# Splitting gate's weight pairs while val's values are scanned, folding the second block from the first slot, and a smaller background share

## The chip, the cores and the metric

The kernel runs on one core of a Trainium2 chip. The metric is device microseconds of one execution; the kernel before has a median of 902.73 us over three runs (901.56 to 907.99).

## What is computed

Attention with a local mask in half of the heads and a strided mask in the other half gives 2304 tokens of 512 numbers. Two networks follow, one after the other:

```python
h = x @ w_in                                  # 512 -> 2048
y = (h * np.cos(h)) @ w_out                   # 2048 -> 512
g, val = y @ w_gate, y @ w_val                # 512 -> 1536, twice
out = (g / (1 + np.exp(-g)) * val) @ w_out2   # 1536 -> 512
```

The weights come as 64-bit floats. A product is made of three 16-bit matmuls, high x high, high x low and low x high, so every weight and every activation is first scaled by a power of two and split into a high and a low 16-bit half. The scale of a whole matrix must be known before its first piece can be split, so each matrix is read twice: a scan for its largest magnitude, then the split.

## The kernel before, in words

The tokens are in five blocks of 512, 512, 512, 384 and 384. The attention comes first (about 110 us). The first network then goes tile by tile, 16 tiles of 128 hidden columns in each block; I call the 80 tiles **slots** 0 to 79. In slot s TensorE (PE) runs the projection of tile s (`up1`, 12 matmuls into a PSUM bank) and one or two contractions of earlier tiles (`down1`, 12 matmuls each). The lag between them falls from 12 tiles to 2 over slots 14 to 39, and in slots 17, 19, 22, 24, 27, 29, 32, 34, 37 and 39 two contractions are run. For each tile VectorE (DVE) has two fixed operations: L577 (in the slot after the projection) and L584 (in the slot after that), which frees the bank. The banks are four. At the end of a block, DVE and ScalarE (ACT) move the four sums out of PSUM (L555 and L557).

Everything else that DVE, ACT and GpSimd (POOL) do in these slots is **background work** for the second network. It lies in one first-in first-out list (`fill`); each entry has a cost in us, and `pump` takes entries while a credit lasts that each slot refills with a share of (PE work of the slot - 1.25): `SHARE` in blocks 0 and 1, `SHARE2` after. Work on the scales and splits of the activations goes through a second list, `urgent`, one piece at each call of `pump_urgent`. The background work, in order:

- split of w_out (`direct_later`), scan of the twelve tiles of w_gate (L174), scan of the twelve of w_val (L174), each followed by `top_later`;
- `open_weights`: from the slot on in which the lag and the storage allow it, `scale_later` for both matrices, then `pair_later` for six pairs of tiles. A pair has a gate half and a val half (`pair_half`). For each half two tiles are converted (L224 on ACT, L231 and L235 on DVE), POOL forms four combinations of the two (L915), and the results are split into a high half (L245, ACT) and a low half (L248, DVE) and stored to DRAM (L863, from the SP queue). The last of seven results is shared by gate and val. The storage is eight **units**, `unit_free`, handed round in the order in which they come free;
- scan of w_out2, its scale, its split (`seven_later`).

A scale is found in `common_scale` (L136 on PE, L137 on DVE): a 128x128 matmul spreads the column maxima over the partitions into a PSUM bank of the same ring of four that `up1` uses, and DVE reduces it. The engines take their instructions in program order, so what stands behind L137 on DVE, or behind L136 on PE, waits with it.

The second network takes 30 slots of its own (`slots`, six of each block). Its operand is **folded** first: `fold_pieces` makes sums of quarters of the block (L611) and splits seven operands (L245, L248), eight pieces in the `urgent` list. For block 1 they are put there at the end of its second slot (j == 1 of block 0), and three calls of `pump_urgent` in each slot take them from slot 2 of this network on.

Of the kernel before, what the change touches and what calls it, by code (L numbers as in the profile page):

```python
# [58 lines left out]
XM = 5  # L59
HOMES, LATE, UNIT = 24, 4, 16  # L60
W7S = 3
SHARE, SHARE2, SB = 0.95, 0.85, 2


WHERE = [((q, c), (3 + q, c)) if q < 3 else ((6, 0), (6, 256))
# [14 lines left out]
def build(tc, qk_l, qk_s, v_l, v_s, w_in, w_out, w_gate, w_val, w_out2, mask_l, mask_s, eye32, eye16, out):  # L80
    nc = tc.nc
    wide = w_in.dtype != F32
    with ExitStack() as ctx:
# [65 lines left out]
        for k, a in MATS.items():  # L149
# [1 line left out]
        scale_w = {}  # L151

        order = deque([("in", j) for j in range(M1)] + [("out", j) for j in range(M1)] * 2
                      + [(mat, j) for mat in ("gate", "val") for j in range(M2)]
                      + [(mat, 2 * j + i) for j in range(NPR) for mat in ("gate", "val") for i in range(2)]
                      + [("out2", j) for j in range(M2)] * 2)

        def load_raw():
# [85 lines left out]
        def hi_part(dst, src, s):  # L244
            nc.scalar.activation(out=dst, in_=src, func=AF.Copy, scale=s)  # L245

        def lo_part(dst, src, s, hi):
            nc.vector.scalar_tensor_tensor(out=dst, in0=src, scalar=s, in1=hi, op0=ALU.mult, op1=ALU.subtract)  # L248
# [31 lines left out]
        def scan_later(mat, j, cost=0.63):  # L280
            later(cost, lambda: scan_raw(mat, j))
# [3 lines left out]
        def top_later(mat):  # L285
            begin([])
            later(0.6, lambda: tops.__setitem__(mat, spread_tops(parts_w[mat], wide)))

        def scale_later(mat, bound):
            later(0.6, lambda: scale_w.__setitem__(mat, common_scale(tops[mat], bound)))  # L290
# [571 lines left out]
        def store_home(j, q, i):  # L862
            nc.sync.dma_start(out=w7_d[j][:, q], in_=homes[i])  # L863
            unit_free.append(i)
# [3 lines left out]
        def flush_after():  # L868
            while after:
                begin(after.popleft())  # L870

        def pair_later(j):

            last = {}
            for mi, mat in enumerate(("gate", "val")):
                pair_half(j, mi, mat, last)

            def hi():
                last["h"] = unit_free.popleft()
                for mi, mat in enumerate(("gate", "val")):  # L880
                    c = slice(256 * mi, 256 * mi + 256)
                    hi_part(homes[last["h"]][:, 0, c], last["f"][:, c], scale_w[mat][0])

            def lo():
                h = homes[last["h"]]
                for mi, mat in enumerate(("gate", "val")):
                    c = slice(256 * mi, 256 * mi + 256)
                    lo_part(h[:, 1, c], last["f"][:, c], scale_w[mat][0], h[:, 0, c])
                unit_free.append(last["i"])
                store_home(j, 6, last["h"])  # L890

            after.append([(0, hi), (1.0, lo)])

        def pair_half(j, mi, mat, last):
            at, f, to = {}, {}, {}
            left, right = slice(0, 256), slice(256, 512)

            def place(q):
                at[q] = unit_free.popleft()
                f[q] = as_f32(homes[at[q]])  # L900
                return f[q]

            def combine(k):
                if k == 0:
                    place(2)
                if k == 3 and not mi:
                    last["i"] = unit_free.popleft()
                    last["f"] = as_f32(homes[last["i"]])
                op, out, a, b = (
                    lambda: (ALU.add, f[2][:, left], f[1][:, left], f[1][:, right]),  # L910
                    lambda: (ALU.subtract, f[1][:, left], f[0][:, left], f[1][:, left]),
                    lambda: (ALU.subtract, f[2][:, right], f[2][:, left], f[0][:, left]),
                    lambda: (ALU.subtract, last["f"][:, 256 * mi:256 * mi + 256], f[0][:, right], f[2][:, right]),
                )[k]()
                nc.gpsimd.tensor_tensor(out=out, in0=a, in1=b, op=op)  # L915

            def hi(q):
                to[q] = unit_free.popleft()
                hi_part(homes[to[q]][:, 0], f[q], scale_w[mat][0])

            def lo(q):
                h = homes[to[q]]
                lo_part(h[:, 1], f[q], scale_w[mat][0], h[:, 0])
                unit_free.append(at[q])
                store_home(j, 3 * mi + q, to[q])

            for q in range(2):
                steps = conv_steps(mat, 2 * j + q, lambda q=q: place(q), False)[1]
                begin(steps + [(0, lambda k=k: combine(k)) for k in range(4)] * q)
                if not q:  # L930
                    flush_after()
            parts = [[(0, lambda q=q: hi(q)), (0.7, lambda q=q: lo(q))] for q in range(3)]
            begin(parts[0])
            after.extend(parts[1:])

        def open_weights(lag):

            if lag + 4 <= UNIT:
                most[0] = UNIT
            if not opened and most[0] == UNIT and max(taken, default=0) < UNIT:  # L940
                opened.append(True)
                scale_later("gate", TW_IN)
                scale_later("val", TW_IN)
                for j in range(NPR):
                    pair_later(j)
                flush_after()
                begin([])
                later(0, lambda: None, "pairs")
                for i in range(M2):
                    scan_later("out2", i, 1.0)  # L950
                top_later("out2")
            if len(opened) == 1 and lag < LATE and max(taken, default=0) < LATE:
                opened.append(True)
                most[0] = LATE
                for i in range(3):
                    later(1.0, lambda: None)
                scale_later("out2", TW_LAST)
                seven_later()
# [2 lines left out]
        for j in range(M1):  # L961
            direct_later("out", j, wo)
        direct_end()
        for mat in ("gate", "val"):
            for j in range(M2):
                scan_later(mat, j, 1.7)
            top_later(mat)
        urgent = deque()

        def urge(pieces, key=None):  # L970
# [188 lines left out]
            return p  # L1159

        px = open_slot(0)
        for s, (blk, j) in enumerate(slots):
            n = BLOCKS[blk][1]
            h = n // 2
# [33 lines left out]
            py = halves(pacc.tile([128, 512], F32, name=f"acc{KC - 1}"), h)  # L1198
            multiply(1, w, x, py, h, True)
            join(0, 0, py, a)  # L1200
            if last:
                piece_sums(last)
                his, los = second_set(last)
                run(his)
            pz = halves(bank(), h)
            multiply(4, w, x, pz, h, True)
            b = snap(pz)
            if last:
                run(los)
            pump_urgent()  # L1210
# [26 lines left out]
            pump_urgent()  # L1237
            multiply(3, w, x, old, h, False)
            nc.scalar.activation(out=c["C"][1][:, :, 0:h], in_=old, func=AF.Copy)
            if j == 1 and blk + 1 < NBLK:  # L1240
                urge(fold_pieces(blk + 1, sy, ys, spans), ("ys", blk + 1))
            if blk == 1 and j == 2:
                urge(late_scale)
# [78 lines left out]
```

## Time and profile before

| | us |
|---|---|
| median of three runs | 902.73 |
| the profiled execution, whole | 904.13 |
| its span, first to last instruction | 902.2 |
| PE busy in the span | 862.4 |
| DVE busy | 691.8 |
| ACT busy | 521.2 |
| POOL busy | 199.3 |

The span is what the views below cut up; the 1.9 us around it are not the kernel's instructions. Busy times are sums over stretches with different limits. In a row of the timeline the first number is the start in us from the span's start, the second the duration; a bracket gives the idle time of that engine just before and what ended it.

### The profile page before, as it was taken

To read this page: it belongs to the slowest core of one execution; us is meant where nothing else is said; L and a number is where in the kernel's file an instruction comes from. 1 tells how busy PE (TensorE), PEld (TensorE's weight loads), DVE (VectorE), ACT (ScalarE), POOL (GpSimd) and SP (SyncE) were. 2 spreads that over 40 slices of the span, in tenths; PEclk is the share of its full clock that TensorE was granted. 3 is DMA by queue.
4 is the path that set the end of the run, shared out by engine and by line. 5 is a ranking of instruction groups with operands and counts; after the bars stand their busy time and mean duration, and the time that the engine had idled before them with its cause. 6 is when DMAs were issued, how large, how long until landed. Compare 5 with 4: busy or idle time off the path is not lost.

```text
span 902.2 us, 18542 instructions
## 1 busy us (share of the span) xinstructions
PE 862.4 (96%) x7228; PEld 609.8 (68%) x7228; DVE 691.8 (77%) x1337; ACT 521.2 (58%) x1046; POOL 199.3 (22%) x253
## 2 busy tenths in 40 slices
PE   7999999989999979899999998899999999999998
PEld 4776644434444434455655686788888899999998
DVE  4797989896758999869988378857886776776672
ACT  4787988763445667547887355536444444544440
POOL 3342414121234656522322200000000000000000
PEclk8897999999999989999999999999999999999999
DMA  9997751568545675651645344657677687888894
GB/s 302 352 304 219 249 187 48 163 189 272 191 144 197 214 241 178 225 204 49 215 136 198 156 151 177 247 200 265 233 255 267 216 273 284 299 290 309 317 330 148
DMA packets 53512, 200.61 MB, mean 222 GB/s; under 512 B 5456, under 2 KB 16208, under 8 KB 49584
## 3 DMA queue, kind: packets, MB, share of 16 engines
q1 hardware_dynamic: 53424, 199.42, 64.8%
q8 instruction: 57, 0.93, 0.5%
q14 instruction: 31, 0.25, 0.1%
HBM read 175.41 MB, written 23.99 MB: 221 GB/s over the span
## 4 chain that ended last, share of the span: by engine, by line
PE 66%; DVE 10%; ACT 7%; DMA 6%; issue 6%; POOL 4%; SPq 0%; POOLq 0%; ACTq 0%; DVEq 0%
PE acc L693 14%; PE bank L541 10%; PE bank L543 10%; PE bank L542 10%; PE acc L541 5%; PE acc L543 5%; PE acc L542 5%; DMA vl<-v_l 3%; PE bank L435 2%; DVE arena L248 2%; POOL arena L915 2%; POOL arena L589 2%; PE po L488 2%; ACT arena L245 2%; DMA v_pair<-v_s 1%
## 5 line engine op out<-in xcount | busy, mean ns | idle before, releaser
L541 PE MATMUL bank<-xs,wi 128*128 128x256 f16 (+3 forms) x780 | 233.8, 300 | 22.1 <-DVE tb L584 9.1
L543 PE MATMUL bank<-xs,wi 128*128 128x256 f16 (+3 forms) x780 | 234.1, 300 | 0.0
L542 PE MATMUL bank<-xs,wi 128*128 128x256 f16 (+3 forms) x780 | 233.9, 300 | 0.0
L589 POOL TENSOR_TENSOR arena<-tb,arena 128x512 f16<-128x512 f32 (+1 forms) x80 | 91.7, 1148 | 240.6 <-ACT arena L588 205.7
L542 PEld LDWEIGHTS <-wi 128*128 128x128 f16 x880 | 86.2, 98 | 62.5 <-issue 30.2
L541 PE MATMUL acc<-arena 128*128 128x512 f16 (+1 forms) x320 | 114.7, 358 | 0.0
L542 PE MATMUL acc<-arena 128*128 128x512 f16 (+1 forms) x320 | 114.5, 358 | 0.0
L543 PE MATMUL acc<-arena 128*128 128x512 f16 (+1 forms) x320 | 114.5, 358 | 0.0
L541 PEld LDWEIGHTS <-wi 128*128 128x128 f16 x880 | 86.3, 98 | 38.4 <-issue 4.1
L543 PEld LDWEIGHTS <-wi 128*128 128x128 f16 x880 | 86.3, 98 | 35.6 <-issue 1.4
L693 PEld LDWEIGHTS <-arena 128*128 128x128 f16 x1080 | 100.7, 98 | 8.2
L678 POOL TENSOR_TENSOR wi<-tb 128x256 f32<-128x256 f32 (+1 forms) x30 | 20.2, 675 | 347.5 <-DVE tb L659 347.5
L663 ACT ACTIVATE arena<-tb 128x256 f16<-128x256 f32 (+3 forms) x59 | 28.9, 489 | 115.3 <-DVE tb L659 111.6
L574 ACT ACTIVATE tb<-bank,quarter,c 128x512 int32<-128x512 f32 (+1 forms) x75 | 54.4, 725 | 49.5 <-PE bank L543 36.9
L542 PEld LDWEIGHTS <-arena 128*128 128x128 f16 x600 | 58.8, 98 | 35.0 <-issue 2.5
L693 PE MATMUL acc<-arena 128*128 128x256 f16 (+1 forms) x702 | 82.0, 265 | 0.0
L543 PEld LDWEIGHTS <-arena 128*128 128x128 f16 x600 | 58.7, 98 | 33.0 <-issue 0.2
L541 PEld LDWEIGHTS <-arena 128*128 128x128 f16 x600 | 58.8, 98 | 32.8 <-ACT arena L588 0.3
L658 DVE SCALAR_TENSOR_TENSOR tb<-tb,arena 128x512 f32<-128x512 f32 (+1 forms) x60 | 38.0, 634 | 44.9 <-ACT tb L652 44.8
L588 ACT ACTIVATE arena<-tb 128x512 f16<-128x512 f32 (+1 forms) x80 | 46.5, 581 | 35.4 <-PE acc L543 32.4
L541 PE MATMUL bank<-xs,arena 128*128 128x256 f16 (+1 forms) x240 | 62.9, 262 | 1.7 <-DVE arena L1190 1.2
L543 PE MATMUL bank<-xs,arena 128*128 128x256 f16 (+1 forms) x240 | 62.9, 262 | 0.0
(146 smaller groups left out, 1734.5 us busy)
## 6 DMA issues: line engine op xcount, KB each, us to landing
wi<-w SPq DMA_DIRECT2D x20, 1792.0 KB
arena<-w SPq DMA_DIRECT2D x60, 576.0 KB, 5.3
raw<-w_out SPq DMA_DIRECT2D x56, 512.0 KB, 4.0
arena<-w SPq DMA_DIRECT2D x10, 1792.0 KB
raw<-w_gate SPq DMA_DIRECT2D x24, 512.0 KB, 4.6
raw<-w_val SPq DMA_DIRECT2D x24, 512.0 KB, 4.4
w<-arena SPq DMA_DIRECT2D x42, 256.0 KB, 2.1
raw<-w_in SPq DMA_DIRECT2D x16, 512.0 KB
```

The costliest lines, as they stand in the source:

```text
L245: nc.scalar.activation(out=dst, in_=src, func=AF.Copy, scale=s)
L248: nc.vector.scalar_tensor_tensor(out=dst, in0=src, scalar=s, in1=hi, op0=ALU.mult, op1=ALU.subtract)
L541: nc.tensor.matmul(out=o, lhsT=w[:, 0, c], rhs=x[0], start=first, stop=False, **kw)
L542: nc.tensor.matmul(out=o, lhsT=w[:, 0, c], rhs=x[1], start=False, stop=False, **kw)
L543: nc.tensor.matmul(out=o, lhsT=w[:, 1, c], rhs=x[0], start=False, stop=last, **kw)
L574: nc.scalar.activation(out=c["w"].bitcast(I32), in_=c["ph"], func=AF.Identity, scale=turn[c["blk"]], bias=quarter)
L588: nc.scalar.activation(out=g[:, 0, 0:n], in_=w, func=AF.Copy)
L589: nc.gpsimd.tensor_tensor(out=g[:, 1, 0:n], in0=w, in1=g[:, 0, 0:n], op=ALU.subtract)
L658: nc.vector.scalar_tensor_tensor(out=t, in0=t, scalar=1.0, in1=gate, op0=ALU.add, op1=ALU.mult)
L663: nc.scalar.activation(out=to, in_=src, func=AF.Copy, scale=2.0 ** -11)
L678: nc.gpsimd.tensor_tensor(out=t_sums[:, 0, 0:h], in0=c["t"][0][:, h:2 * h], in1=c["t"][0][:, 0:h], op=ALU.subtract)
L693: nc.tensor.matmul(out=o[:, c], lhsT=w[:, 256 * i + 128 * c:256 * i + 128 * c + 128], rhs=unit(u)[:, x:x + h], start=j == c == i == 0, sto ...
```

## The change

1. `load_raw`'s order and the background list: w_val is no longer scanned ahead of the opening. When the opening comes, gate's scale is found and gate's six halves are split, with one val scan put after the first and one after the second tile of each half; then val's scale, then val's six halves.
2. `half_later` takes the place of `pair_later` and `pair_half`: the seventh result of a pair is split and stored for gate and for val apart (256 columns each; six more stores).
3. The fold of block 1 is put in `urgent` before the first slot of the second network, and that slot has three more calls of `pump_urgent`.
4. `SHARE2` goes from 0.85 to 0.75.

```diff
-SHARE, SHARE2, SB = 0.95, 0.85, 2
+SHARE, SHARE2, SB = 0.95, 0.75, 2
...
-                      + [(mat, j) for mat in ("gate", "val") for j in range(M2)]
-                      + [(mat, 2 * j + i) for j in range(NPR) for mat in ("gate", "val") for i in range(2)]
+                      + [("gate", j) for j in range(M2)]
+                      + [(mat, j) for j in range(M2) for mat in ("gate", "val")] + [("val", j) for j in range(M2)]
...
+            def last_hi():
+                last["h"] = unit_free.popleft()
+                hi_part(homes[last["h"]][:, 0, mine], last["f"][:, left], scale_w[mat][0])
+
+            def last_lo():
+                h = homes[last["h"]]
+                lo_part(h[:, 1, mine], last["f"][:, left], scale_w[mat][0], h[:, 0, mine])
+                unit_free.append(last["i"])
+                nc.sync.dma_start(out=w7_d[j][:, 6, :, mine], in_=h[:, :, mine])
+                unit_free.append(last["h"])
+
             for q in range(2):
                 steps = conv_steps(mat, 2 * j + q, lambda q=q: place(q), False)[1]
                 begin(steps + [(0, lambda k=k: combine(k)) for k in range(4)] * q)
                 if not q:
                     flush_after()
+                elif beside:
+                    scan_later(beside, 2 * j)
             parts = [[(0, lambda q=q: hi(q)), (0.7, lambda q=q: lo(q))] for q in range(3)]
             begin(parts[0])
-            after.extend(parts[1:])
+            if beside:
+                scan_later(beside, 2 * j + 1)
+            after.extend(parts[1:] + [[(0, last_hi), (0.5, last_lo)]])
...
                 scale_later("gate", TW_IN)
+                for j in range(NPR):
+                    half_later(j, 0, "gate", "val")
+                flush_after()
+                top_later("val")
                 scale_later("val", TW_IN)
                 for j in range(NPR):
-                    pair_later(j)
+                    half_later(j, 1, "val")
...
-        for mat in ("gate", "val"):
-            for j in range(M2):
-                scan_later(mat, j, 1.7)
-            top_later(mat)
+        for j in range(M2):
+            scan_later("gate", j, 1.7)
+        top_later("gate")
...
         px = open_slot(0)
+        urge(fold_pieces(1, sy, ys, spans), ("ys", 1))
...
             join(0, 0, py, a)
+            if not s:
+                pump_urgent()
+                pump_urgent()
...
             b = snap(pz)
+            if not s:
+                pump_urgent()
...
-            if j == 1 and blk + 1 < NBLK:
+            if j == 1 and 0 < blk < NBLK - 1:
```

The instructions themselves show where things go. Before, on DVE in slot 30, the scales of gate and val are found one behind the other (s_3308 is gate's, s_3317 val's; parts and xy belong to the block scales), and the first conversion of a gate tile follows:

```order
L112 RECIPROCAL s_3308<-q 128x1
L113 TENSOR_SCALAR inv_3309<-q 128x1
L114 TENSOR_SCALAR s_3308<-s_3308 128x1
L137 TENSOR_REDUCE q<-bank 128x1
L112 RECIPROCAL s_3317<-q 128x1
L113 TENSOR_SCALAR inv_3318<-q 128x1
L114 TENSOR_SCALAR s_3317<-s_3317 128x1
L231 TENSOR_SCALAR arena<-arena 128x512
L577 SCALAR_TENSOR_TENSOR tb<-bank,c_2528,tb 128x512
```

Now gate's scale stands in slot 25, and val's in slot 34, on DVE behind a scan, four low halves and L584. This is DVE's slot 34 (s_3609 is a block scale that stands in slot 34 before too, s_3057 gate's, s_3646 val's):

```order
L577 SCALAR_TENSOR_TENSOR tb<-bank,c_3439,tb 128x512
L137 TENSOR_REDUCE q<-bank 128x1
L112 RECIPROCAL s_3609<-q 128x1
...
L174 TENSOR_REDUCE pw_val<-raw 128x1
L248 SCALAR_TENSOR_TENSOR arena<-arena,s_3057 128x512 x2
L584 SCALAR_TENSOR_TENSOR tb<-tb,bank 128x512
L248 SCALAR_TENSOR_TENSOR arena<-arena,s_3057 128x512
L248 SCALAR_TENSOR_TENSOR arena<-arena,s_3057 128x256
...
L137 TENSOR_REDUCE q<-bank 128x1
L112 RECIPROCAL s_3646<-q 128x1
```

The two moved: from slot 30, where they stood together, gate's scale went five slots up and val's four slots down, with the whole of gate's split between them.

In the second network, DVE's first slot before (L1190 adds two products, L658 and L659 make the gated value, L666 a low half):

```order
L1190 TENSOR_TENSOR arena<-acc_5710,cv 128x2x256
L521 TENSOR_REDUCE parts_3_5174<-xy_69 128x1
L1190 TENSOR_TENSOR arena<-bank,cv 128x2x256
L120 TENSOR_REDUCE m<-parts_3_5174 128x1
L128 TENSOR_SCALAR p<-m 128x1
L130 TENSOR_SCALAR tops<-id_76,p 128x128
L1190 TENSOR_TENSOR arena<-bank,cv 128x2x256
L658 SCALAR_TENSOR_TENSOR tb<-tb,arena 128x512
```

and the same slot now, where the additions are L1188:

```order
L1188 TENSOR_TENSOR arena<-acc_5716,cv 128x2x256
L521 TENSOR_REDUCE parts_3_5177<-xy_69 128x1
...
L130 TENSOR_SCALAR tops<-id_76,p 128x128
L137 TENSOR_REDUCE q<-bank 128x1
...
L611 TENSOR_TENSOR wi<-xy_67 128x512
L1188 TENSOR_TENSOR arena<-bank,cv 128x2x256
L611 TENSOR_TENSOR wi<-xy_67,wi 128x512
L248 SCALAR_TENSOR_TENSOR xs<-xy_67,s_4477,xs 128x512
L1188 TENSOR_TENSOR arena<-bank,cv 128x2x256
L658 SCALAR_TENSOR_TENSOR tb<-tb,arena 128x512
```

A block scale that was spread over slots 0 and 1 is now whole in slot 0, and the first pieces of the fold stand between the additions of slot 0.

## Rows read from the trace of the kernel before

**Rows 1.** The page, part 1: busy us of each engine, share, instructions.

```profile
PE 862.4 (96%) x7228; PEld 609.8 (68%) x7228; DVE 691.8 (77%) x1337; ACT 521.2 (58%) x1046; POOL 199.3 (22%) x253
```

**Rows 2.** Windows: length, busy of PE, PEld, DVE, ACT, POOL, granted clock, DMA, GB/s.

```profile
226.98:285.15 58.17, 57.47 (x268) 26.11 (x267) 40.40 (x76) 27.80 (x46) 17.52 (x19) 1.00 0.53 183
233.03:260.44 27.41, 27.08 (x128) 12.35 (x127) 18.79 (x41) 11.07 (x19) 6.38 (x5) 1.00 0.52 192
285.15:381.17 96.02, 84.44 (x386) 38.01 (x386) 90.22 (x136) 64.44 (x108) 58.56 (x56) 0.96 0.61 206
331.00:335.00 4.00, 4.00 (x11) 1.37 (x10) 3.97 (x8) 4.00 (x8) 3.38 (x4) 0.55 0.80 265
```

**Rows 3.** Waits of PE: us in total, times, longest.

```profile
PE bank L541 <- DVE tb L584: 9.1, 6, 3.0
PE bank L541 <- DVE q L137: 6.6, 8, 3.0
```

**Rows 4.** Timeline of PE: first matmul of slots 26, 35, 41, 50 and 52.

```profile
226.98 0.38 PE L541 MATMUL bank<-xs,wi 128*128 128x512 f16 x1
...
285.15 0.38 PE L541 MATMUL bank<-xs,wi 128*128 128x512 f16 x1 [0.38 <-DVE q L137]
...
330.87 0.58 PE L541 MATMUL bank<-xs,wi 128*128 128x512 f16 x1 [3.03 <-DVE q L137]
...
381.17 0.33 PE L541 MATMUL bank<-xs,wi 128*128 128x384 f16 x1
...
390.85 0.32 PE L541 MATMUL bank<-xs,wi 128*128 128x384 f16 x1 [0.38 <-DVE q L137]
```

**Rows 5.** Timeline of DVE: around the openings of slots 26, 40 and 52.

```profile
231.06 0.75 DVE L555 TENSOR_SCALAR xy<-acc,c 128x512 f32<-128x512 f32 x1 [6.64 <-PE acc L543]
...
233.03 0.74 DVE L577 SCALAR_TENSOR_TENSOR tb<-bank,c,tb 128x512 f32<-128x512 f32 x1
...
329.87 0.74 DVE L577 SCALAR_TENSOR_TENSOR tb<-bank,c,tb 128x512 f32<-128x512 f32 x1
...
330.53 0.28 DVE L137 TENSOR_REDUCE q<-bank 128x1 f32<-128x128 f32 x1
...
396.25 0.61 DVE L577 SCALAR_TENSOR_TENSOR tb<-bank,c,tb 128x384 f32<-128x384 f32 x1
```

**Rows 6.** Groups of DVE by line and form, 260 to 375 us: count, busy, mean ns.

```profile
L248 DVE SCALAR_TENSOR_TENSOR arena<-arena,s 128x512 f16<-128x512 f32 x36 | 35.3, 993 | 6.6 <-ACT arena L245 6.3
L235 DVE SCALAR_TENSOR_TENSOR arena<-raw,arena 128x512 int32<-128x512 int32 x24 | 21.2, 882 | 0.7
L231 DVE TENSOR_SCALAR arena<-arena 128x512 int32<-128x512 int32 x24 | 14.7, 613 | 1.6 <-ACT arena L224 1.6
...
L584 DVE SCALAR_TENSOR_TENSOR tb<-tb,bank 128x512 f32<-128x512 f32 x16 | 10.8, 676 | 0.0
L248 DVE SCALAR_TENSOR_TENSOR arena<-arena,s 128x256 f16<-128x256 f32 x11 | 6.6, 637 | 0.0
```

**Rows 7.** Groups of DVE by line and form, 200 to 260 us: val's scan.

```profile
L174 DVE TENSOR_REDUCE pw_val<-raw 128x1 f32<-128x512 f32 x12 | 7.8, 675 | 0.0
```

**Rows 8.** Timeline of POOL and DVE: a low half beside POOL, one without.

```profile
322.55 3.87 POOL L915 TENSOR_TENSOR arena<-arena 128x256 f32<-128x256 f32 x4
322.57 1.26 DVE L248 SCALAR_TENSOR_TENSOR arena<-arena,s 128x512 f16<-128x512 f32 x1
...
327.49 0.74 DVE L248 SCALAR_TENSOR_TENSOR arena<-arena,s 128x512 f16<-128x512 f32 x1
```

**Rows 9.** Timeline of DVE: first addition of the second network's slots 2, 5, 6.

```profile
538.84 0.68 DVE L1190 TENSOR_TENSOR arena<-acc,cv 128x512 f32<-128x512 f32 x1
...
574.76 0.68 DVE L1190 TENSOR_TENSOR arena<-acc,cv 128x512 f32<-128x512 f32 x1
...
584.57 0.68 DVE L1190 TENSOR_TENSOR arena<-acc,cv 128x512 f32<-128x512 f32 x1
```

**Rows 10.** The page, part 6: stores of split weights, KB each, us to landing.

```profile
w<-arena SPq DMA_DIRECT2D x42, 256.0 KB, 2.1
```

More of the change, by code (lines that the diff above doesn't have):

```diff
@@ L870, in flush_after, with half_later @@
                 begin(after.popleft())
[L872 to L895, printed above, removed]
+        def half_later(j, mi, mat, beside=None):
+            at, f, to, last = {}, {}, {}, {}
             left, right = slice(0, 256), slice(256, 512)
+            mine = slice(256 * mi, 256 * mi + 256)
             def place(q):
@@ L905, in combine @@
                     place(2)
-                if k == 3 and not mi:
+                if k == 3:
                     last["i"] = unit_free.popleft()
@@ L912, in combine @@
                     lambda: (ALU.subtract, f[2][:, right], f[2][:, left], f[0][:, left]),
-                    lambda: (ALU.subtract, last["f"][:, 256 * mi:256 * mi + 256], f[0][:, right], f[2][:, right]),
+                    lambda: (ALU.subtract, last["f"][:, left], f[0][:, right], f[2][:, right]),
                 )[k]()
```

## The prediction

> **What bounds the kernel now.** I read the page's busy times first: PE is busy for 862.4 of 902.2 us [rows 1], so all that any change of order can win is some 40 us, and only where PE waits. The waits of PE come next: they name DVE, by L584 (the bank of an older tile is not free yet, 9.1 us in all) and by L137 (a scale is being found in a bank that the next projection needs, 6.6 us) [rows 3]. Third, the timeline of PE, cut at the first matmul of a slot, says where [rows 4]. Slots 26 to 34 take from 226.98 to 285.15, 58.17 us with PE busy for 57.47 [rows 2]: nine projections and thirteen contractions (four slots have two), 22 groups of 12 matmuls, so a group of 512 columns takes 57.0 / 22 = 2.59 us, after two waits for scales. Slots 35 to 49 are thirteen projections and fifteen contractions of 512 columns and two projections of 384 (slots 48 and 49 contract 512-column tiles still): 28 x 2.59 + 2 x (1.94 + 2.59) = 81.6 us. They took 96.0 [rows 2, 4]. These 14.4 us are the largest loss of the kernel. DVE is busy for 90.2 of them. In the 27 us before the first split of a gate pair, 233 to 260, it is busy for 18.8 only [rows 2]. So the idle DVE time lies ahead of the split, the late DVE behind it.
>
> The reader should also see how a wait for L137 differs from one for L584. With four banks PE can run about two slots ahead of DVE. At a scale it cannot: the next projection takes the bank that L137 reads. At slot 41 PE starts at 330.87, right behind L137, which ran from 330.53 to 330.81 because DVE opened slot 40 (L577) only at 329.87 [rows 4, 5]. Whatever DVE is late at L137, PE pays at once.
>
> **The change, part by part.**
>
> *Slots 26 to 34.* DVE opens slot 26 at 233.03, behind L555, for which it has waited 6.64 us for PE [rows 5]. Gate's scale in slot 25 makes PE wait for L137 once, 0.4 us as at 285.15 [rows 4]; the conversion and the scan that follow it fit into the 6.64 us. So slot 26 opens at 233.5. From there to val's scale in slot 34 the order has 100 operations on DVE where the kernel before had a light load: 21 low halves or splits of 512 columns at 0.993, 6 of 256 at 0.637, 11 L231 at 0.613, 11 L235 at 0.882, 9 L584 at 0.676 [rows 6], 9 L577 at 0.74 [rows 5], 11 scans and 4 maxima of the same shape at 0.675 [rows 7], and 18 of a column or a 128-column tile at some 0.2. That is 20.9 + 3.8 + 6.7 + 9.7 + 6.1 + 6.7 + 10.1 + 3.6 = 67.6 us. Each starts a little before the one ahead of it has ended (L137 starts 0.66 after an L577 of 0.74 [rows 5]): 100 x 0.07 = 7.0 off.
>
> The means are those of a stretch in which POOL is busy for 58.6 of 96 us [rows 2], and a low half takes 1.26 beside POOL's combinations, 0.74 without [rows 8]. In slots 26 to 34 POOL will have about 20 combinations (0.97 each [rows 8]) and nine low parts of tiles, some 31 of 62 us. The lengthening in the 67.6 is 18 x 0.25 + 22 x 0.19 = 8.7 us at most (taking the same excess for L231 and L235); with POOL at 50% in place of 61% it is 1.5 less. DVE's waits for ACT and POOL inside such work were 96.0 - 90.2 = 5.8 us in fifteen slots [rows 2], so 3.5 in nine. In all 67.6 - 7.0 - 1.5 + 3.5 = 62.6 us: L137 of val ends at 296.1, and slot 35 starts there, not at 285.15. **Cost: +10.9.** Bounds: no lengthening and no waits gives 52 us and a start of slot 35 at 285.6 (+0.5); full lengthening and 6 us of waits gives +15. I take the middle since these instructions, in this order of conversion, combination and low half, are those of the rows.
>
> On this the Trainium skill has a rule that speaks against the change: by "SBUF — State Buffer", section "Who interferes with whom", a DVE instruction with two SBUF inputs and a POOL instruction that reads SBUF exclude one another for a whole instruction, while a reduction never takes part. The row of 1.26 beside 0.74 agrees, and val's scans show the same 0.675 as gate's do. By the rule the scans keep 0.675 beside the combinations, as summed above; if they were lengthened like the low halves, it would be 11 x 0.25 = 2.8 us more.
>
> *Slots 35 to 49.* By the order and these prices some 11 us of DVE's splitting are gone from here, and PE's wait at val's scale lets DVE catch up, so slots 35 and 36 cost nothing. But a DVE that is not late must wait again for PE at L555, in slot 37, which has two contractions: as in slot 26, L577 follows PE's last contraction by about 0.9 us, so DVE opens slot 37 some 8.6 us after PE does. In slots 37 to 39 DVE has 21.0 us of work by the same prices and overlap and PE 20.7, so it opens slot 40 as late, and L137 there ends 1 us later: 8.6 + 1.0 - 5.2 = 4.4, with the 0.4 of the two matmuls 4.8 us of waiting (before, this is the place of the 3.03 in [rows 4], with a wait for a bank just ahead of it). After that DVE has 4.4 to 5.2 us in a slot of 5.2 and is not late by two slots again. A wait of this length costs clock too: after the one that ended at 330.87 PE ran at a granted 0.55 for 4 us [rows 2], half speed, 1.8 us lost. I take that once. 81.6 + 4.8 + 1.8 = 88.2 in place of 96.0: **gain 7.8.** Bounds: 14.4 if neither wait comes, 5 if both cost clock.
>
> *Slots 50 to 79.* `SHARE2` thins the background: the same work, three slots longer, ending in slot 76, ahead of the second network, so it moves no end. But the scale of w_out2 moves from slot 54 to 52, the slot that DVE opens late behind L555: it opens at 396.25, 5.4 us after PE's 390.85 [rows 4, 5]; with L577 and a maximum ahead, L137 ends 1.5 us later, and PE's slot takes 4.5. PE waits 2.4 where it waited 0.4. Lighter slots after that may give back 1 of the small waits. **+1.0**, from -2 to +2.5.
>
> *The second network.* Slots 2, 3 and 4 hold the fold's eight pieces and take 574.76 - 538.84 = 35.9 us, the next slot without a piece 9.8 [rows 9]: 6.5 us for eight pieces, 0.8 each. Now three lie in slot 0, where DVE still waits for PE, three in slot 1 and two in slot 2. I count the first three as won, 2.4 us, and the others as they were. Against that, the scale in slot 0 stands between two products: PE waits for its maxima, and the last addition of slot 0 comes behind L611 and L248 (1.4 us); 0.6 and 0.9 us. **-0.9**, from -4 to +2.
>
> The six more stores are of 128 KB; a store of 256 KB lands in 2.1 us [rows 10], and SP does not bound anything here. Nothing is counted for them.
>
> *Sum:* 10.9 - 7.8 + 1.0 - 0.9 = +3.2 us on the profiled execution's 904.13, which gives 907.3. That execution was 1.4 over the median of the runs; on the median, 902.73 + 3.2 is, rounded, 906 us.
>
> **The rivals.** *Faster: the idle time swallows the split.* DVE has 8.6 idle us between 233 and 260 [rows 2], plus what it waits at L555. If the converted tiles run at their short durations, val's L137 ends at 285.6 and the first term is +0.5: 0.5 - 7.8 + 1.0 - 0.9 = -7.2, so 895.5; with the fold at its best, 892.4. For it: POOL is less busy there. Against it: 52 us of DVE work is still all that PE has time for, with no wait for POOL at all, and such waits are in the rows [rows 6].
>
> *Slower: the units go round too fast.* A half now takes eight units where a pair took fourteen, and there are eight. POOL's first combination and ACT's conversion then wait for a store to land, 2.1 us [rows 10], with DVE queued behind them, in each of the five halves before val's scale. At 1.5 us a half that is +7.5 on the first term, paid at once at L137: 913.4. It decides from about 1 us a half on. For it: waits of ACT and POOL are on the chain already [rows 6]. Against it: stores are half as many per us.
>
> *No change in all:* the same DVE work is only shifted, the two stretches cancel, and the fold gives what the scale of w_out2 takes: 903.
>
> **How the numbers follow.** Forecast 0.5, faster rival 0.2, slower rival 0.2, no change 0.1. About 1% (9 us) is what a measurement can tell. Faster by more than that needs the faster rival with the fold's best case, half of it: 0.1. Slower by more is the slower rival's greater part and the forecast's upper edge: 0.2. The rest is 0.7. The range reaches from the faster rival (895.5) to just past the slower one: 895 to 914.
>
> **What would show it.** Right: PE's first matmul of slot 35 comes at 293 to 299 with a wait for L137 of 5 us or more ahead of it; DVE is 90% busy from 233 on; slot 50 comes 2 to 5 us later than 381.17; a wait of 2 us at slot 53; the second network's slots 3 and 4 at 9.8 us. Wrong: no long wait at slot 35, then the first term was never paid and the time is near 895; or waits of L224 and of POOL's combinations for stores, then it is above 912.

## The result and the profile after

The changed kernel takes 908.55 us (median of 15 runs, 906.30 to 912.17) where the kernel before, on the same chip, takes 902.65 (899.39 to 907.99): a ratio of 1.0063, 95% interval 1.0043 to 1.0083. It is slower by 0.6%, inside the 1% that was called no change, and 2.6 us above the forecast. The ratios here and below are formed from undisturbed executions alone, so they differ a little from the ratios of the medians. The profiled execution of after has a span of 904.6 us at a granted clock of 0.983. In the new kernel file the functions named below keep their lines, except POOL's combinations, now L894, and the second network's additions, now L1188.

Page, part 1, of after (answers to [rows 1]):

```profile
PE 858.6 (95%) x7228; PEld 606.8 (67%) x7228; DVE 688.8 (76%) x1337; ACT 522.0 (58%) x1046; POOL 200.0 (22%) x253
```

Each engine has the same number of instructions as before. Nothing was added to it, only the places changed; the SP queue has six more stores to issue.

Before stages are compared, one piece must be set aside. These are the windows of the attention (from the start to slot 1), of before and then of after: length, busy of PE, PEld, DVE, ACT, POOL, granted clock, DMA, GB/s.

```profile
0.00:117.77 117.77, 109.55 (x1527) 74.80 (x1528) 90.07 (x247) 89.82 (x320) 41.69 (x86) 0.88 0.89 286
```

```profile
0.00:112.88 112.88, 104.61 (x1527) 71.58 (x1528) 90.05 (x247) 89.12 (x320) 41.62 (x86) 0.92 0.93 299
```

The code is the same here, the counts are the same, and the granted clock is not: 0.88 and 0.92. In the profiles of the twelve runs below slot 1 begins between 112.88 and 125.68, whatever was edited. So these 4.9 us say nothing on the change, and I count from slot 1 on. There before takes 902.2 - 117.77 = 784.4 us and after 904.6 - 112.88 = 791.7: 7.3 us more, to set beside 5.9 between the medians.

Windows of after: slots 26 to 34, 35 to 49, and slot 41 alone (answer to [rows 2]):

```profile
222.65:293.00 70.35, 58.04 (x267) 25.97 (x267) 64.89 (x105) 40.72 (x67) 34.97 (x34) 0.98 0.76 254
293.00:383.36 90.36, 86.32 (x387) 38.66 (x387) 73.89 (x122) 52.36 (x85) 40.50 (x39) 0.94 0.57 193
335.46:343.20 7.74, 7.74 (x25) 2.95 (x25) 5.32 (x10) 3.51 (x5) 4.71 (x5) 0.66 0.77 260
```

Slots 26 to 34 went from 58.17 us to 70.35, with PE busy for 58 in both; slots 35 to 49 from 96.02 to 90.36. DVE's load has moved as the change says: 40.4 to 64.9 us in the first stretch, 90.2 to 73.9 in the second. Cut at the first matmul of a slot:

| stretch | before | after | difference |
|---|---|---|---|
| slots 1 to 25 | 109.21 | 109.77 | +0.56 |
| slots 26 to 34 | 58.17 | 70.35 | +12.18 |
| slots 35 to 49 | 96.02 | 90.36 | -5.66 |
| slots 50 to 78 | 119.31 | 119.99 | +0.68 |
| slot 79 to the end | 401.72 | 401.25 | -0.47 |

PE's waits in after (answer to [rows 3]): us in total, times, longest.

```profile
PE bank L136 <- DVE tops L130: 10.0, 3, 8.7
PE bank L541 <- DVE q L137: 8.3, 7, 3.4
PE bank L541 <- DVE tb L584: 7.6, 6, 2.3
```

A new name leads the list: PE waits at L136, the matmul that spreads the maxima, for the operand that DVE makes at L130. The timeline of PE shows the first matmuls of slots 26 and 34, the longest wait, at the end of slot 34, and the first matmuls of slots 35, 41, 50 and 53 (answer to [rows 4]):

```profile
222.65 0.38 PE L541 MATMUL bank<-xs,wi 128*128 128x512 f16 x1 [0.38 <-DVE q L137]
...
276.22 0.38 PE L541 MATMUL bank<-xs,wi 128*128 128x512 f16 x1 [0.38 <-DVE tb L584]
...
283.99 0.22 PE L136 MATMUL bank<-tops,ones 128*128 128x128 bf16 x1
292.94 0.27 PE L136 MATMUL bank<-tops,ones 128*128 128x128 bf16 x1 [8.73 <-DVE tops L130]
293.00 0.63 PE L541 MATMUL bank<-xs,wi 128*128 128x512 f16 x1
...
335.46 0.58 PE L541 MATMUL bank<-xs,wi 128*128 128x512 f16 x1 [3.43 <-DVE q L137]
...
383.36 0.33 PE L541 MATMUL bank<-xs,wi 128*128 128x384 f16 x1
...
399.76 0.32 PE L541 MATMUL bank<-xs,wi 128*128 128x384 f16 x1 [1.97 <-DVE q L137]
```

And this is DVE's opening of slot 26, and its slot 34 from the opening to val's scale:

```profile
228.69 0.74 DVE L577 SCALAR_TENSOR_TENSOR tb<-bank,c,tb 128x512 f32<-128x512 f32 x1
...
283.98 0.75 DVE L577 SCALAR_TENSOR_TENSOR tb<-bank,c,tb 128x512 f32<-128x512 f32 x1
284.64 0.28 DVE L137 TENSOR_REDUCE q<-bank 128x1 f32<-128x128 f32 x1
...
285.23 0.68 DVE L174 TENSOR_REDUCE pw_val<-raw 128x1 f32<-128x512 f32 x1
285.82 1.25 DVE L248 SCALAR_TENSOR_TENSOR arena<-arena,s 128x512 f16<-128x512 f32 x1
289.24 1.24 DVE L248 SCALAR_TENSOR_TENSOR arena<-arena,s 128x512 f16<-128x512 f32 x1 [2.17 <-ACT arena L245]
290.40 0.68 DVE L584 SCALAR_TENSOR_TENSOR tb<-tb,bank 128x512 f32<-128x512 f32 x1
291.00 1.14 DVE L248 SCALAR_TENSOR_TENSOR arena<-arena,s 128x512 f16<-128x512 f32 x2
...
292.63 0.25 DVE L130 TENSOR_SCALAR tops<-id,p 128x128 bf16<-128x128 bf16 x1
293.24 0.29 DVE L137 TENSOR_REDUCE q<-bank 128x1 f32<-128x128 f32 x1 [0.36 <-PE bank L136]
```

Read the two together. PE comes to the block's scale at 283.99, and DVE answers at 284.64: at this point DVE is hardly late, since PE has just spent 7.8 us on slot 34, a projection and two contractions. The 8.73 us that follow are the rest of DVE's list for this one slot (the last scan, four low halves and a small one, L584, and 2.17 us for ACT), which stands ahead of val's maxima. PE has 5.2 us of its own work ready for slot 35 and may not begin it.

### The profile page after: what moved, and what is told of

Its sections match the earlier page's. It is cut to its first block, busy times and chain, and to the rows that moved or that the text cites. A ratio compares the mean times of both kernels' runs of the same rounds, so it can differ in the third digit from the quotient of the medians.

```text
span 904.6 us, 18561 instructions
## 1 busy us (share of the span) xinstructions
PE 858.6 (95%) x7228; PEld 606.8 (67%) x7228; DVE 688.8 (76%) x1337; ACT 522.0 (58%) x1046; POOL 200.0 (22%) x253
## 3 DMA queue, kind: packets, MB, share of 16 engines
q1 hardware_dynamic: 55824, 199.42, 64.6%
## 4 chain that ended last, share of the span: by engine, by line
PE 68%; DVE 13%; ACT 6%; issue 5%; DMA 5%; POOL 2%; SPq 0%; ACTq 0%; POOLq 0%; DVEq 0%
PE acc L693 14%; PE bank L541 11%; PE bank L542 10%; PE bank L543 10%; PE acc L541 6%; PE acc L543 6%; PE acc L542 6%; DMA vl<-v_l 3%; DVE arena L248 2%; PE bank L435 2%; PE po L488 2%; DMA v_pair<-v_s 1%; DVE tb L577 1%; DVE cv L235 1%; DVE tb L584 1%
## 5 line engine op out<-in xcount | busy, mean ns | idle before, releaser
L541 PE MATMUL bank<-xs,wi 128*128 128x256 f16 (+3 forms) x780 | 234.3, 300 | 18.3 <-DVE q L137 8.3
L589 POOL TENSOR_TENSOR arena<-tb,arena 128x512 f16<-128x512 f32 (+1 forms) x80 | 92.7, 1160 | 251.5 <-ACT arena L588 225.7
L541 PEld LDWEIGHTS <-wi 128*128 128x128 f16 x880 | 86.3, 98 | 46.3 <-issue 12.2
L541 PE MATMUL acc<-arena 128*128 128x512 f16 (+1 forms) x320 | 114.6, 358 | 0.0
L541 PEld LDWEIGHTS <-arena 128*128 128x128 f16 x600 | 58.8, 98 | 32.7 <-issue 0.3
L658 DVE SCALAR_TENSOR_TENSOR tb<-tb,arena 128x512 f32<-128x512 f32 (+1 forms) x60 | 38.0, 633 | 45.0 <-ACT tb L652 45.0
L588 ACT ACTIVATE arena<-tb 128x512 f16<-128x512 f32 (+1 forms) x80 | 46.5, 582 | 39.5 <-PE acc L543 37.2
L541 PE MATMUL bank<-xs,arena 128*128 128x256 f16 (+1 forms) x240 | 62.8, 262 | 4.4 <-ACT cv L1184 3.8
```

Of the source, the lines that this page charges most:

```text
L541: nc.tensor.matmul(out=o, lhsT=w[:, 0, c], rhs=x[0], start=first, stop=False, **kw)
L588: nc.scalar.activation(out=g[:, 0, 0:n], in_=w, func=AF.Copy)
L589: nc.gpsimd.tensor_tensor(out=g[:, 1, 0:n], in0=w, in1=g[:, 0, 0:n], op=ALU.subtract)
L658: nc.vector.scalar_tensor_tensor(out=t, in0=t, scalar=1.0, in1=gate, op0=ALU.add, op1=ALU.mult)
```

## The experiments

The kernel before, run beside them, took 901.90 us in the first set (35 runs), 900.69 in the second (11), 902.04 in the third (29) and 902.47 in the last (17). Stages are compared from slot 1 on, as above.

**1. The split of the pairs alone.** The kernel after, with the fold and `SHARE2` of before:

```diff
-SHARE, SHARE2, SB = 0.95, 0.75, 2
+SHARE, SHARE2, SB = 0.95, 0.85, 2
...
-        urge(fold_pieces(1, sy, ys, spans), ("ys", 1))
...
```

> The kernel after with the old fold and SHARE2 0.85: only the order of scans and gate halves is changed. Theory (val's scale in slot 34 stops PE while DVE is late): the wait for the scale's maxima in slot 34 is 8 to 11 us, and the time is 908 to 913 us, ratio to before 1.006 to 1.012, slightly above the kernel after because blocks 2 and later keep the larger share. Rival (the smaller share is what cost the time): ratio 1.000 to 1.003.

Measured: 907.42 us, ratio 1.0065 (1.0034 to 1.0096). The split alone costs as much as the whole change. Its wait for val's maxima is 5.48 us, less than the 8 to 11 expected, but PE has lost more ahead of it (1.83 and 2.37 us for banks, before slots 31 and 32); slots 26 to 34 take 69.2 us in all.

**2. The fold alone.** The kernel before, with the new fold:

```diff
+        urge(fold_pieces(1, sy, ys, spans), ("ys", 1))
...
+            if not s:
+                pump_urgent()
+                pump_urgent()
...
-            if j == 1 and blk + 1 < NBLK:
+            if j == 1 and 0 < blk < NBLK - 1:
```

> The kernel before with the fold of block 1 begun in the first slot of the second network, nothing else. Theory: ratio 0.997 to 1.001, the fold gives about 1 us; the second network's slots 3 and 4 take 9.8 us instead of 12, slots 0 and 1 about 1 and 2.5 us more. Rival (the new place of the scale in slot 0 costs as much as it gives): 1.000 to 1.003.

Measured: 901.02 us, ratio 0.9982 (0.9955 to 1.0009): not to be told from no change by itself. Its stretch from slot 79 on takes 0.4 us less: the second network's slots 3 and 4 take 9.7 us each, and slots 0 and 1 1.5 and 2.7 us more, as expected.

**3. A smaller share alone.** The kernel before with `SHARE2` at 0.80:

```diff
-SHARE, SHARE2, SB = 0.95, 0.85, 2
+SHARE, SHARE2, SB = 0.95, 0.80, 2
```

> The kernel before with SHARE2 0.80 in place of 0.85 (the scans, the pairs and the fold as before). Theory: slots 32 to 47 carry less background while DVE is the late engine there, so slots 35 to 49 take 92 to 95 us in place of 96, and the ratio is 0.995 to 0.999. Rival (the wait only moves to the next scale): 1.000 to 1.003.

Measured: 900.19 us, ratio 0.9983 (0.9946 to 1.0020), again not to be told from 1. Slot 40 takes 10.0 us instead of 11.2, and slots 50 to 54 22.0 instead of 22.6. Slots 35 to 49 take 95.2 us, just above the 92 to 95 expected.

**4. No scale for val.** The kernel after; val's values are scanned still, and val is split with gate's scale:

```diff
-                top_later("val")
-                scale_later("val", TW_IN)
+                begin([])
+                later(0, lambda: scale_w.__setitem__("val", scale_w["gate"]))
```

> The kernel after, but val is split with gate's scale: its maxima are still scanned, but no matmul and no reduction for val's own scale are made. This takes out the wait in slot 34 and nothing else. Theory: the wait of 8.7 us for the maxima is gone, what stays in slot 34 is about 1 us for the block's scale; DVE is still late, so slot 40 waits 5 to 6 us; time 901 to 905, ratio 0.999 to 1.003. Rival (PE is bound by DVE's sum of work, so the wait goes to the banks instead): ratio 1.005 to 1.008, as the kernel after.

Measured: 898.02 us, ratio 0.9974 (0.9943 to 1.0005), faster than either theory had it; ahead of slot 41 PE waits 3.6 us where 5 to 6 were expected. Slot 35 now begins here:

```profile
286.00 0.38 PE L541 MATMUL bank<-xs,wi 128*128 128x512 f16 x1 [0.63 <-DVE q L137]
```

Eight small DVE instructions and a matmul are gone, some 1.5 us of DVE's list by the rows above, and with them some 8 to 10 us of time (ratios 1.0063 and 0.9974; 908.55 beside a before of 902.65, 898.02 beside 901.90). Slots 26 to 34 take 62.7 us. So of the 12.2 that they had lost, 7.6 hang on val's scale, and 4.5 stay: waits of 2.15 and 2.04 us for L584 ahead of slots 31 and 32, which DVE's load itself makes.

**5 to 8. Scales without PE.** If the barrier is what costs, a scale that doesn't pass through a PSUM bank should cost nothing. In run 5 val's maxima go to DRAM and come back on all partitions, by two transfers of the SP queue, and DVE reduces them; run 6 does this for val and for the blocks' scales, run 7 for the blocks' scales in the kernel before, run 8 for these with the new fold and `SHARE2` 0.80.

```diff
+            far = tc.dram_tile([128, 1], F32, name=f"far{count[0]}")
+            row = small.tile([128, 128], F32, name="row", bufs=1)
+            nc.sync.dma_start(out=far, in_=p)
+            nc.sync.dma_start(out=row, in_=far.rearrange("p a -> (a p)").partition_broadcast(128))
...
+            nc.vector.tensor_reduce(out=p, in_=row, op=ALU.max, axis=AX.X)
```

> The kernel after with val's own scale, but spread over the partitions by two small DMAs through DRAM instead of a matmul into a bank, and reduced on DVE after the first two val tiles are converted. Nothing on PE waits for it. Theory: as the run with gate's scale for val, a ratio to before of 0.995 to 1.000, with no PE wait above 2 us in slot 34. Rival (what that run won came from val's scale being left out, not from PE's wait): ratio 1.004 to 1.008.

> The run before in this list, with the scales of the blocks (from the second on, and of the first network's results) found the same way. Theory: the waits for L137 in slots 40, 52 and 68 and the clock lost behind the first go too, some 4 to 8 us; DVE stays late, so part comes back as waits for banks: ratio 0.986 to 0.994. Rival (each wait for a scale only shifts into waits for banks): 0.995 to 1.000, the same as the run with val's scale alone.

> The kernel before with the blocks' scales found by DMA, gate's and val's scales left on PE in slot 30. Theory: the wait of 5.7 us in slot 40 and the slow clock behind it go, and waits for banks take part of it: ratio 0.992 to 0.997. Rival (they only move): 0.998 to 1.001.

> The kernel before with the new fold, SHARE2 0.80 and the blocks' scales by DMA: the old order of scans and pairs with all else that helped. Theory: 0.988 to 0.995. If it is slower than the run with all scales by DMA in the new order, splitting gate early is worth something once no scale stops PE; if it is as fast or faster, the new order is worth nothing.

Measured: 912.84 us, ratio 1.0132 (1.0087 to 1.0177); 965.64, 1.0697 (1.0659 to 1.0734); 962.06, 1.0653 (1.0614 to 1.0693); 956.08, 1.0592 (1.0557 to 1.0628). All four are far off. SP's queue and DVE in run 5, around val's scale:

```profile
297.48 0.45 SPq L155 DMA_DIRECT2D far<-p  x1
305.21 0.32 SPq L156 DMA_DIRECT2D row<-far  x1
```

```profile
309.63 0.29 DVE L161 TENSOR_REDUCE q<-row 128x1 f32<-128x128 f32 x1 [9.41 <-DMA row<-far]
```

The second transfer starts 7.7 us after the first, which it has to wait for, and DVE, which takes its instructions in order, stands still for 9.41 us with everything behind the reduction. PE then waits for a bank ahead of slot 37 (L608 is L584 in this file):

```profile
310.95 0.59 PE L565 MATMUL bank<-xs,wi 128*128 128x512 f16 x1 [9.66 <-DVE tb L608]
```

Slots 26 to 34 take 62.3 us in run 5, as in run 4 (62.7), and here val has its own scale. So what run 4 won in these slots comes from PE's wait, and not from the scale's being left out. In run 6, the waits of DVE:

```profile
DVE q L161 <- DMA row<-far: 81.9, 9, 11.4
```

Nine waits, 81.9 us of a DVE that has no such time. The barrier was only moved from PE to the engine that PE waits for.

**9. The parts without the split.** The kernel before, with the new fold of run 2 and `SHARE2` 0.80 of run 3.

> The kernel before with the new fold and SHARE2 at 0.80, no split of pairs, all scales as they were. If the gains of the fold (0.9982) and of the share (0.9983) come from different places, as their stages say (the second network's first slots; slot 40), they add: ratio 0.9965, 899.5 us. Rival: they share one cause (DVE late in slots 40 to 79 and what it passes on), and the ratio stays at 0.998. The sum is wanted at 0.995 to 0.998.

Measured: 896.62 us, ratio 0.9944 (0.9918 to 0.9970). That is a little below the 0.995 to 0.998 expected. The sum, 0.9965, lies inside the interval and the rival's 0.998 outside, so the gains add as far as this run can tell; from slot 1 on the profiles have 0.6 us for the fold, 2.3 for the share and 3.5 for both. It is the lowest ratio measured, and faster than both kernels. Its largest wait for a scale stands ahead of slot 41 still:

```profile
330.04 0.59 PE L541 MATMUL bank<-xs,wi 128*128 128x512 f16 x1 [4.63 <-DVE q L137]
```

**10 and 11. The same work, another place for val's scale.** In both the kernel after has val's scans spread 3, 3, 2, 2, 2 and 0 over gate's six halves, and makes val's maxima ahead of the last half. In run 10 the scale comes right behind L577 of slot 33 and the block's maxima, in run 11 right behind L577 of slot 34, just ahead of the block's scale. The last three lines are run 11's; run 10 hangs the scale on the first piece of `urgent` instead, and nothing else differs between the two:

```diff
+TOP_AT = 5
+VAL_AT = [[0, 1, 2], [3, 4, 5], [6, 7], [8, 9], [10, 11], []]
...
+                    if j == TOP_AT:
+                        later(0.6, lambda: tops.__setitem__("val", spread_tops(parts_w["val"], wide)))
+                        later(0, beside_block)
                     half_later(j, 0, "gate", "val")
                 flush_after()
-                top_later("val")
-                scale_later("val", TW_IN)
...
+            cost, fn, key = urgent[1]
+            val = lambda: scale_w.__setitem__("val", common_scale(tops["val"], TW_IN))
+            urgent[1] = (cost + 0.6, lambda: (val(), fn()), key)
```

> The kernel after, but val's scans are put 3, 3, 2, 2, 2, 0 to the six gate halves, its maxima are made ahead of the last half, and its scale stands in slot 33 right behind L577 (before the block's scale, which stays in slot 34). The same DVE work, another place of the scale. Theory: PE pays what DVE is late at L137. In slot 33 of the kernel after, L577 starts at 279.36 and PE's slot ends at 276.2, so the wait is about 4 us instead of 8.7: 4 to 5 us less than the kernel after, 904 us, ratio 1.001. Rival: PE is held by the sum of DVE's work in slots 26 to 35 wherever the scale stands (L584's banks); then the wait only changes its name and the time stays at 907 to 909.

> As the run with the scale in slot 33, but val's scale stands in slot 34, right behind L577 and beside the block's scale. Theory: in the kernel after, slot 34's block scale opened its L137 at 284.64, 0.4 us after PE came to it, since this slot has two contractions; with val's scale beside it the wait is about 1 us, so that 7 to 8 us of the 8.7 go: ratio 0.997 to 0.999, 900 to 901 us, like the run without val's scale. Rival: the late DVE work is paid in slots 35 to 37 through L584 instead, and the time is 905 or more.

Measured: run 10 904.71 us, ratio 1.0058 (1.0033 to 1.0084); run 11 900.33, ratio 0.9970 (0.9942 to 0.9997). Lines stand three higher in these files (L139 is L137, L138 is L136, L544 is L541, L580 is L577). PE at val's scale in run 10:

```profile
278.84 0.22 PE L138 MATMUL bank<-tops,ones 128*128 128x128 bf16 x1 [2.25 <-DVE tops L132]
...
282.20 0.59 PE L544 MATMUL bank<-xs,wi 128*128 128x512 f16 x1 [3.14 <-DVE q L139]
```

PE and then DVE in run 11:

```profile
288.20 0.22 PE L138 MATMUL bank<-tops,ones 128*128 128x128 bf16 x1
288.80 0.22 PE L138 MATMUL bank<-tops,ones 128*128 128x128 bf16 x1 [0.38 <-DVE q L139]
289.40 0.38 PE L544 MATMUL bank<-xs,wi 128*128 128x512 f16 x1 [0.38 <-DVE q L139]
```

```profile
286.11 0.75 DVE L580 SCALAR_TENSOR_TENSOR tb<-bank,c,tb 128x512 f32<-128x512 f32 x1
288.45 0.29 DVE L139 TENSOR_REDUCE q<-bank 128x1 f32<-128x128 f32 x1 [1.60 <-PE bank L138]
```

In run 10 the wait is 2.25 + 3.14 = 5.4 us, above the 4 expected because the maxima themselves came late, and slots 26 to 34 take 68.1 us. By its ratio the run cannot be told from the kernel after, though its median is only 0.3% over the 902.04 beside it: it decides little between theory and rival. In run 11 PE waits 0.38 twice, and it is DVE that waits for PE, 1.60 us. Slots 26 to 34 take 63.4 us, nearly what they took with no scale at all (62.7). The rival, that the work of the stretch holds PE wherever the scale stands, falls: runs 10 and 11, with the same work and beside the same before, lie apart by 0.9% (1.0058 and 0.9970), and the kernel after by as much from run 11 (1.0063).

**12. All of it together.** Run 11 with `SHARE2` 0.80.

> Val's scale in slot 34 beside the block's, the split of gate's pairs, the new fold, and SHARE2 at 0.80 in place of 0.75. What is asked: with the scale's wait gone, is the split itself worth anything over the run that has the fold and SHARE2 at 0.80 without it (0.9944)? By the stages, slots 14 to 35 take 139.4 us with the split against 133.6 without, and slots 35 to 79 at SHARE2 0.75 207.8 against 212.3; about 1.5 us of the 24.2 of slots 50 to 55 should go at 0.80. The two sums are then alike: 0.994 to 0.998, 897 to 900 us. Rival: the thinner backlog of DVE after slot 40 gives more, and it is under 0.992.

Measured: 902.81 us, ratio 1.0011 (0.9984 to 1.0038): a miss on the other side of both theories. PE's waits at val's scale and at slot 40's scale:

```profile
289.45 0.22 PE L138 MATMUL bank<-tops,ones 128*128 128x128 bf16 x1 [2.00 <-DVE q L139]
...
334.53 0.59 PE L544 MATMUL bank<-xs,wi 128*128 128x512 f16 x1 [4.36 <-DVE q L139]
```

They were 0.38 and 3.43 in run 11. DVE comes later to both barriers: slots 34, 35, 40 and 42 to 44 take 1.6, 1.6, 1.6 and 2.4 us more than in run 11, slots 26 to 33 and 50 to 78 2.2 and 1.6 less. That the larger share makes DVE late there is likely, but one profile of each does not show it. 0.75 looks like the better share with the split, though the two intervals overlap a little (0.9942 to 0.9997 and 0.9984 to 1.0038), and I had added stages of runs that don't add. Whether the mended split is worth anything beside run 9 stays open: 0.9970 and 0.9944 have intervals that overlap.

## Why the prediction was right, and where its sizes were off

The direction was forecast and the range held. The size was not met so well: +3.2 us was the sum, +5.9 lie between the medians and +7.3 between the profiles from slot 1 on, and three of the four terms came out dearer than forecast.

*Slots 26 to 34, forecast +10.9.* Measured 0.56 + 12.18 = +12.7 from slot 1 on, with a wait of 8.7 us at val's scale (for the maxima ahead of L136, and not for L137) and slot 35's first matmul at 293.00, just within the 293 to 299 given; DVE is busy for 64.89 of the 70.35 us, 92%. The way of working holds: DVE's list from the opening of slot 26 to val's L137 was worked out at 62.6 us, and it took from 228.69 to 293.24, 64.6. Groups of DVE by line and form in that stretch (answer to [rows 6, 7]):

```profile
L248 DVE SCALAR_TENSOR_TENSOR arena<-arena,s 128x512 f16<-128x512 f32 x18 | 17.5, 983 | 2.6 <-ACT arena L245 2.6
L235 DVE SCALAR_TENSOR_TENSOR arena<-raw,arena 128x512 int32<-128x512 int32 x11 | 10.2, 930 | 0.3
L231 DVE TENSOR_SCALAR arena<-arena 128x512 int32<-128x512 int32 x11 | 7.7, 697 | 0.1
L174 DVE TENSOR_REDUCE pw_val<-raw 128x1 f32<-128x512 f32 x11 | 7.4, 676 | 0.0
...
L248 DVE SCALAR_TENSOR_TENSOR arena<-arena,s 128x256 f16<-128x256 f32 x6 | 2.9, 476 | 0.0
```

The low halves kept 0.98 us, while L235 and L231 took 0.93 and 0.70 where 0.88 and 0.61 were used: the 1.5 us that I took off for a less busy POOL were not there. The scans took 676 ns here and 675 before [rows 7]: of the eleven, six ran beside a POOL instruction for 0.5 us or more and took 673 to 679 ns, the five beside none 672 to 680. That is what the Trainium skill's "SBUF — State Buffer", section "Who interferes with whom", says of a reduction, and the extra 2.8 us that were weighed against it did not come.

What the step did not see is how much of the sum hangs on one place. It reads the wait as lateness that nine slots gather. But DVE opens slot 26 6.0 us after PE (228.69 and 222.65) and slot 34 7.8 us after (283.98 and 276.22): on the way it fell behind by 1.7 us more, while PE waited 3.6 us for L584. The two contractions of slot 34 cover the 7.8, and what PE then waits for is DVE's list of that one slot. Runs 4 and 11 show that most of the wait goes when the scale is left out or stands at the head of the slot. The load of the nine slots costs 4.5 to 5.2 us (runs 4 and 11); the other 7.0 to 7.6 are the place of one scale in the list of one slot.

*Slots 35 to 49, forecast 88.2 in place of 96.0.* Measured 90.36, a gain of 5.7 and not 7.8. The forced wait at L555 and the late scale of slot 40 came as worked out: DVE opens slots 37 and 40 8.6 us after PE, and PE waits 0.61 + 3.43 us where 4.8 were forecast. The term that was mis-sized is the clock, "I take that once" at 1.8 us. It is lost twice: slot 35 takes 6.82 us instead of 5.2 behind the 8.7 us wait (its first matmuls 0.63 us each where 0.38 is usual), and slot 41 7.74, at a granted 0.66 in the window above.

*Slots 50 to 79, forecast +1.0.* Slot 50 starts at 383.36, 2.2 us after [rows 4], within the 2 to 5 given, but that is luck: counted from slot 1 it comes 7.1 later. From there it is +0.7, with 1.97 us at slot 53 for the 2.4 forecast. *The second network, forecast -0.9.* Measured -0.5. The first additions of slots 0 to 5 (answer to [rows 9]):

```profile
520.75 0.69 DVE L1188 TENSOR_TENSOR arena<-acc,cv 128x512 f32<-128x512 f32 x1 [1.62 <-PE acc L543]
...
533.53 0.68 DVE L1188 TENSOR_TENSOR arena<-acc,cv 128x512 f32<-128x512 f32 x1
...
545.92 0.68 DVE L1188 TENSOR_TENSOR arena<-acc,cv 128x512 f32<-128x512 f32 x1
...
557.90 0.68 DVE L1188 TENSOR_TENSOR arena<-acc,cv 128x512 f32<-128x512 f32 x1
...
567.57 0.68 DVE L1188 TENSOR_TENSOR arena<-acc,cv 128x512 f32<-128x512 f32 x1
...
577.24 0.68 DVE L1188 TENSOR_TENSOR arena<-acc,cv 128x512 f32<-128x512 f32 x1
```

Slots 3 and 4 take 9.7 us, as forecast. Slot 0 takes 12.8 us where the kernel before took 11.3 (its additions stand at 517.88 and 529.17): the 1.5 more are what was counted for the scale and the last addition, so by this sum nothing is left for its three pieces, and they are won as counted. The five pieces in slots 1 and 2 (12.4 and 12.0 us beside 9.7) cost 1.0 each where 0.8 was used, and that is why the gain is smaller.

*The rivals.* The faster one asked whether DVE's idle time swallows the split. With the scale in the kernel after's place it does not; in run 11's place over half of it is swallowed (5.2 us are left of 12.2, where this rival had 0.5), which the prediction did not think of, since it took the scale's place in the list as given. Of the slower one, units that go round too fast, the wait is there, on ACT, in slots 26 to 34 of after (a store of 256 KB lands in 3.2 us in after's page, 2.1 in [rows 10]):

```profile
ACT arena L224 <- DMA w<-arena: 10.4, 8, 2.8
```

DVE's waits for ACT are 2.6 us in all there, far from the 1.5 us a half that this rival had. But 2.17 of them stand in slot 34, at 289.24, inside the wait of PE. The rows of ACT and POOL lead back from there to a store:

```profile
282.20 0.68 ACT L224 ACTIVATE arena<-raw 128x512 f32<-128x512 f32 x1 [2.25 <-DMA w<-arena]
...
288.49 1.40 ACT L245 ACTIVATE arena<-arena,s 128x512 f16<-128x512 f32 x2 [3.19 <-POOL arena L894]
```

```profile
285.37 1.15 POOL L589 TENSOR_TENSOR arena<-tb,arena 128x512 f16<-128x512 f32 x1 [4.15 <-ACT arena L588]
```

ACT waits 2.25 us for the store and comes late to L588; POOL's L589 waits for that, with the combination behind it; ACT's L245 waits for the combination, and DVE for L245. So up to 2.2 of the 8.73 us may be this rival's. That is read from the rows of one profile; no run tries it.

## What to carry to other kernels

Where an engine must answer another in the middle of its list, what counts is what stands ahead of the answer in that slot, and not only how busy the engine is over the stage: make the operand a slot earlier and put the answer at the head of a slot in which the asking engine has the most work of its own (run 11: slot 34, two contractions; run 10, in slot 33 with one, gained little or nothing). Sum a moved load over the stage, as here, but then check the row at the last barrier for how late the engine already is when the slot begins. A scale that went round by DRAM was no way out here, since DVE stood at the reduction for 9 us each time with its list behind it; whether the reduction would cost nothing much later in that list was not tried.

## What was not expected of the hardware

A transfer of 0.5 KB, 128 partitions with one number each, took 7.7 us from its issue to its landing beside the other stores of the SP queue (median of ten in run 6), and its way back of 64 KB 4.5 us, while a store of 256 KB took 2.5 in the same run and 2.1 in the kernel before [rows 10]. How much of the 7.7 is the queue ahead of it and how much the small packets was not tried. And the granted clock of the same attention code differed between profiled executions, 0.88 and 0.92, which moved everything behind it by 4.9 us: as much as what was to be measured.
